# A transformer block on one core: which softmax quads VectorE computes, and the latencies the instruction order is planned with

## The chip, the cores and the metric

The kernel runs on one core of a Trainium2 chip. The metric is the device time of one execution in microseconds (us); less is better. The core has five engines that run side by side, each through its own instruction list in order, and they wait for each other on semaphores: TensorE (PE; its weight loads are listed as PEld), VectorE (DVE), ScalarE (ACT), GpSimd (POOL) and SyncE (SP), which mostly issues DMAs. PE writes its results to PSUM, eight banks of 128 x 512 floats.

## The reference

One pre-norm transformer block on a sequence of 2048 with 640 features, 32 heads of 20:

```python
qkv = layernorm(x) @ wqkv                     # 640 -> 3*640
p   = softmax(q @ k.T * 20**-0.5)             # 32 heads, 2048 x 2048 each
h   = x + (p @ v) @ wo
g   = layernorm(h)
out = h + (gelu(g @ w_gate) * (g @ w_up)) @ w_down   # 640 -> 1728 -> 640
```

The softmax needs 32 x 2048 x 2048 exponentials, and that sets the shape of the kernel.

## The kernel before, in words

**Tiles and slots.** Scores are made transposed, with 128 keys on the partitions. A *tile* is 128 x 512 scores (one PSUM bank); a *quad* is four tiles, one for each of four heads (`g` names the group of four heads, `j` the head in it). The queries are cut into eight chunks, of 512, then five of 256, then two of 128 (`SIZES`, line 316). A *slot* is 16 quads, 64 tiles: a head group at all keys for chunk 0, two groups for a chunk of 256, four for one of 128. There are 32 slots: 0 to 7 are chunk 0, 8 to 11 chunk 1, 12 to 15 chunk 2, 16 to 19 chunk 3, 20 to 23 chunk 4, 24 to 27 chunk 5, 28 and 29 chunk 6, 30 and 31 chunk 7.

**Two ways to an exponential.** Most tiles go to ACT: `unit` (line 941) makes the scores of two or three tiles on PE (L965), ACT takes the exponential of them in one instruction (L368, `pts` or `rege` from `ps`), and the quads are multiplied with v on PE (`pv_op`, line 922; in the trace L368, `ps` from `v_all`). Units of three and of two tiles alternate over banks 0 to 2 and 3 to 4. Some quads of each slot, `D_QUADS[slot]` (line 336), are computed on DVE by `d_exp` (line 867): each tile's scores are scaled to a 16-bit integer out of PSUM (L889), and then a group of two tiles ("l", 128 x 1024, slots below 18) or four tiles ("w", 128 x 2048, from slot 18, `D_WIDE`) goes through three one-input passes and two or three two-input passes of bit arithmetic. In the slots of `DA_SLOTS` the last addition is a DMA that accumulates, issued by POOL (line 910).

Which quads these are, and when DVE begins them, is set here:

```python
        n = D_QUADS[s_]
        taken = [quads[len(quads) * (m + 1) // (n + 1)] for m in range(n)]
        rest = [q + (j,) for q in quads if q not in taken for j in range(4)]
        part = D_PART if lead[s_] == 0 else 1.0
        dq += [(max(len(tiles) + ... - lead[s_], dq[-1][0] if dq else 0), q + (j,))
               for m, q in enumerate(taken) for j in range(4)]
```

The taken quads are spread over the slot, and each is begun `lead` (`D_LEAD`, line 338) ACT tiles ahead of its place.

**The rest of a chunk** (`post`, line 1083), once its attention is done: the attention output is transposed (by a DMA on SP, `dma_transposes`, line 621, except for chunk 0 and the last one), multiplied with wo (L667), added to x on DVE (L1105), normalized, transposed again, and put through the gate (PE L1138, copied out of PSUM on DVE by L1173), the gelu in place on ACT (L368, `rege` from `rege`), the up projection (PE L1138) times the gate (DVE L1187), and the down projection (PE L1218) plus h (DVE L1222). The gelu needs another activation table than the exponential, so ACT pauses its exponentials for a gelu, with a table load before and one after it. Chunk 1's gelu is kept for chunk 2's (`MERGE`). The last chunk takes another road (L1160, L1163), as nothing is left beside it.

**The order of the instructions** is written out when the kernel is built. Every operation is recorded with an engine, an estimated duration, an estimated latency (`lat`: from its end to when its result is seen) and a priority, and `Sched.schedule` (line 94) simulates the five engines with these estimates: whenever an engine is free it takes the ready operation of the best priority. Exponentials and their scores have priority 0, the background work (`post`, projections) a worse one. The order that comes out is each engine's program; on the chip each engine keeps that order whatever the real durations are. Where PE would be too little busy, the planner adds matmuls with zero weights (`self.pad`: L368, `ps` from `kt_all,zer`, in groups of four) or idle full-size ones (`self.warm`: `ps` from `kt_all`).

So a change of an estimate changes no work, only the order; a change of `D_QUADS` moves work between ACT and DVE, and the order too.

Of the kernel before, what the change touches and what calls it, by code (L numbers as in the profile page):

```python
# [46 lines left out]
class Sched:  # L47
# [13 lines left out]
    def op(self, eng, fns, dur, prio, reads=(), writes=(), acq=(), rel=(), after=(), sem=None, lat=None, mode=None, util=0.0):  # L61
        if eng == "dve" and rel and prio > self.ev:
            prio = self.ev
        o = Op()
        o.i = len(self.ops)
        o.eng, o.dur, o.lat, o.sem = eng, dur, DRAIN[eng] if lat is None else lat, sem
        o.util = util
        o.mode = mode
        o.tag = writes[0] if writes else None
        o.fns = fns if isinstance(fns, list) else [fns]  # L70
        o.prio = (prio, o.i)
        deps = set(after)
        for r in reads:
            if r in self.lw:
                deps.add(self.lw[r])
        for w in writes:
            if w in self.lw:
                deps.add(self.lw[w])
            deps.update(self.rd.get(w, ()))
        for r in reads:  # L80
            self.rd.setdefault(r, []).append(o.i)
        for w in writes:
            self.lw[w] = o.i
            self.rd[w] = []
        deps.discard(o.i)
        o.deps = deps
        o.acq = list(acq)
        o.rel = list(rel)
        o.succ = []
        o.ready = 0.0  # L90
        self.ops.append(o)
        return o.i
# [237 lines left out]
PV_QUADS = 2  # L330
D_LAG = 8
MERGE = (1,)
DA_ISSUE, DA_LAT = 0.95, 7.0
DA_SLOTS = (1, 2, 3, 5) + tuple(range(9, 32))
PR, PR2 = 12, 6
D_QUADS = (1,) + (2,) * 15 + (2, 2) + (3,) * 10 + (2, 2, 2, 2)
D_FIRST, D_PART = 2, 0.75
D_LEAD = ((0,) * 8, (0, 10, 20) + (42,) * 21)
D_WIDE = 18
RSQRT_MAGIC = float(0x5F3759DF)  # L340

# [1 line left out]
P_QK, P_PV, P_PRO, P_EPI, P_LN, P_BG = 0, 1, 1.5, 2, 2.5, 3  # L343
# [3 lines left out]
def bass_sequential_preLN__mha_block__glu_gated_geglu__prompt_kernel(  # L347
# [12 lines left out]
    with ExitStack() as es:  # L360
        sc = Sched(nc)
        op = sc.op
# [4 lines left out]
        def I(method, *args, **kwargs):  # L367
            return lambda eng: getattr(eng, method)(*args, **kwargs)  # L368
# [64 lines left out]
        wg = carve(NA * DFF).rearrange("p (a f) -> p a f", a=NA)  # L433
        wu = carve(NA * DFF).rearrange("p (a f) -> p a f", a=NA)
# [55 lines left out]
        def cst(fn, key, n=128):  # L490
# [7 lines left out]
           reads=["zer"], writes=["qf1"])  # L498
        op("act", I("activation", f32(qt_all[:, 2, :, :]), zer[:, 0:2].bitcast(FP32).to_broadcast([128, 2048]), ACT.Copy), 1.8, P_QK,
           reads=["zer"], writes=["qf2"])  # L500
        op("act", I("activation", v_all[:, :, :, DH], zer[:, 0:1].unsqueeze(2).to_broadcast([128, NT, H]), ACT.Copy, bias=1.0), 0.5, P_QK,
           reads=["zer"], writes=["vones"])
# [28 lines left out]
        def load(dst, src, key, mb, after=(), writes=None):  # L531
            return op("sp", I("dma_start", dst, src), 0.08, P_BG, writes=writes or [key], after=after,
                      sem=key, lat=mb)
# [85 lines left out]
                   rel=[bk], after=after)  # L619

        def dma_transposes(src, rkeys, dst, wkey, after=()):
            op("sp", I("dma_start_transpose", dst, src), 1.25, P_EPI, reads=rkeys, writes=[wkey], sem=f"xp{wkey[1]}", lat=2.0, after=after)

        _id = [0]

# [114 lines left out]
        def proj_q(t, c, banks, prio, evac="dve"):  # L740
            proj_qk(0, t, c, q_un[:, t, :], ("qu", t), banks, prio, evac)
            if t == 0 and c == 0:
                for j in range(4):
                    q_keys[0][0].append(("q", 0, 0, j))
                    dma(qt_all[32 * j + 1:32 * j + 21, 0, 0, :], q_un[DH * j:DH * j + DH, 0, :], ("q", 0, 0, j),
                        [("qu", 0), "qtm0"], "qc", 2.2, prio - 0.1)
            dma(qdr[c, 128 * t:128 * t + 128, :], q_un[:, t, :], ("qdr", c, t), [("qu", t)], f"qw{t}", 2.7,
                max(prio, P_BG) if t == 0 else prio, 0.4)
            w_readers.append(op("dve", I("tensor_scalar", aq[t].bitcast(I16), q_un[:, t, :].bitcast(I16), 0x7FFF, None,
                                         ALU.bitwise_and), 0.2, prio, reads=[("qu", t)], writes=[aqk(t)]))  # L750

        def q_bound(c, ts, g0, g1, banks, prio):
            bk = Bank(*banks)
            key = ("bk", sc_id())
            for k, t in enumerate(ts):
                w_readers.append(op("pe", lambda eng, k=k, t=t: eng.matmul(
                    bank(bk)[0:32, :], sel[:, t, :], aq[t], start=(k == 0), stop=(k == len(ts) - 1)),
                    c_mm(512), prio, mode="full", util=0.05, reads=[aqk(t), ("sel", t)], writes=[key],
                    acq=[bk] if k == 0 else []))
            op("dve", lambda eng: eng.tensor_scalar(qoff[0:32, :], bank(bk)[0:32, :], OFF, None, ALU.add), c_dve(512), prio,  # L760
               reads=[key], writes=["qoff"], rel=[bk])
            dma(odr[c], qoff[0:32, :], ("odr", c, g0), ["qoff"], "ow", 2.5, prio, 0.4)
            new = [("qo", c, g0)] + [("q", c, g0, j) for j in range(4)]
            for j in range(4):
                dma(qt_all[32 * j + 1:32 * j + 21, c, g0:g1, :],
                    qdr[c].rearrange("(g j e) s -> j e g s", j=4, e=DH)[j, :, g0:g1, :], ("q", c, g0, j),
                    [("qdr", c, t) for t in ts] + q_fills[c], f"q{c}{g0}", 2.5, prio, keep=False)
            dma(qt_all[0:128:32, c, g0:g1, :], odr[c].rearrange("(g j) s -> j g s", j=4)[:, g0:g1, :], ("qo", c, g0),
                [("odr", c, g0)] + q_fills[c], f"q{c}{g0}", 2.5, prio, keep=False)
            for g in range(g0, g1):  # L770
                q_keys[g][c] += new
# [36 lines left out]
        slot_end = []  # L808
        lead = sum(D_LEAD, ())
        for s_, (c, gs) in enumerate(slots):  # L810
            nk = 512 // CHUNKS[c][1]
            quads = [(s_, g, kb) for g in gs for kb in range(NT // nk)]
            n = D_QUADS[s_]
            taken = [quads[len(quads) * (m + 1) // (n + 1)] for m in range(n)]
# [258 lines left out]
        def prefetch(c):  # L1073
            q0, nq = CHUNKS[c]
            nt = nq // 128
            tb = base(c)
            op("sp", I("dma_start", h_sb[:, tb:tb + nt, :], x_hbm[q0:q0 + nq, :].rearrange("(t p) d -> p t d", p=128)), 0.08, P_EPI,
               writes=[("h", tb + tt, hf) for tt in range(nt) for hf in range(2)], sem=f"xr{c}", lat=2.0 + nq * 0.0034,
               after=tuple(e_ops) + tuple(w_readers) if c == 0 else ())
# [167 lines left out]
        for s_, (c, gs) in enumerate(slots):  # L1247
            if c == 0:
                g = s_
                if g + 1 in STEP:  # L1250
                    t, (g0, g1) = g + 1, STEP[g + 1]
                    pr = P_EPI if t == 1 else P_BG
                    proj_q(t, 0, BG0, pr)
                    proj_k(t, BG0, pr)
                    q_bound(0, (t - 1, t), g0, g1, BG0, pr)
                if g < 3:
                    for kt in range(NT * g // 3, NT * (g + 1) // 3):
                        proj_v(kt, 1, BG0, P_BG)
                if g == 5:
                    prefetch(0)  # L1260
                if g >= 5:
                    cc = g - 4
                    for t in range(NA):
                        proj_q(t, cc, BG0, P_BG)
                    q_bound(cc, tuple(range(NA)), 0, NG, BG0, P_BG)
                if g == 7:
                    wr = tuple(w_readers)
                    load(wg, B_w_gate.rearrange("(a p) f -> p a f", p=128), "wg", 11.0, after=wr)
                    load(wu, B_w_up.rearrange("(a p) f -> p a f", p=128), "wu", 16.0, after=wr)
                    load(wd[:, 0:NF - 1, :], B_w_down[0:(NF - 1) * 128, :].rearrange("(a p) d -> p a d", p=128),  # L1270
                         "wd", 21.0, after=wr)
                    r0 = (NF - 1) * 128 - F0[-1]
                    load(wd[r0:128, NF - 1, :], B_w_down[(NF - 1) * 128:DFF, :], "wd", 2.6, after=wr)
                    op(POOL, I("memset", wd[0:r0, NF - 1, :], 0.0), 0.8, P_BG, writes=["wdz", "pool"], after=wr)
            while ui < len(units) and begins[ui] < slot_end[s_]:
                unit(ui)
                ui += 1
            if gs[-1] == NG - 1:
                tail = c == len(CHUNKS) - 1
                sc.ev = P_EV  # L1280
                post(c, ALLB if tail else BGF[c + 1], ALLB if tail else BGC[c + 1], tail)
                if not tail:
                    prefetch(c + 1)
# [30 lines left out]
```

## Time and profile before

| | |
|---|---|
| runs before | 913.15, 915.69, 915.77 us; median 915.69 |
| the profiled execution | 915.13 us, of it the span from the first to the last instruction 913.0 us |
| busy | ACT 871.2 us (95%), PE 832.7 (91%), DVE 763.3 (84%), POOL 134.2 (15%) |
| exponentials on ACT | 356 of 128 x 1536 and 344 of 128 x 1024: 1756 tiles in 700 instructions |
| first exponential, end of the last one | 32.85 us, 876.26 us |
| mean granted TensorE clock | 0.994 of full speed |

A page of the profile has six parts; busy time is the time in which at least one instruction of the engine runs, and an engine that is off the path to the end may idle at no cost. Part 4 follows the chain of work that ended last back from the last instruction, and tells which engine holds it up. Other views give each engine's busy time in chosen stretches, or every instruction in order of time with the idle time before it and what ended it.

The kernel falls in three stages: the first 32 us (loads, first normalization and projections), the loop of exponentials to 876 us with all other work beside it, and a tail of 37 us, in which the last chunk goes through projection, gate, up and down, with what is left over of the chunks before it.

### The profile page before, as it was taken

How to read it: one execution, taken by the hardware profiler on the slowest of the kernel's cores; microseconds unless marked ns; L12 is line 12 of the kernel's file. 1: busy time of each engine (PE TensorE's matmuls, PEld its weight loads, DVE VectorE, ACT ScalarE, POOL GpSimd, SP SyncE). 2: the span in 40 equal slices, each digit the busy share in tenths (PEclk: the TensorE clock that was granted, in tenths of full speed). 3: DMA queues.
4: the chain of work that ended last, by engine and by line, in shares of the span. 5: the costliest groups of instructions: out<-in, count | busy, mean ns of one | idle time of the engine just before them, and what ended most of it. 6: DMA issues, size and time to landing. Idle time of an engine off the chain costs nothing.

```text
span 913.0 us, 25152 instructions
## 1 busy us (share of the span) xinstructions
PE 832.7 (91%) x11135; PEld 383.4 (42%) x11180; DVE 763.3 (84%) x1426; ACT 871.2 (95%) x786; POOL 134.2 (15%) x239
## 2 busy tenths in 40 slices
PE   3999999998897887899998989999999999999998
PEld 2432222222243332334443443344444445666667
DVE  8869989988798985777887989989999998958643
ACT  7999899999999999999999999999999999999971
POOL 5001110000013111111321101031102110203000
PEclk9999999999999999999999999999999999999999
DMA  7213344346304231242422324433353344314300
GB/s 259 84 31 79 79 87 108 96 96 203 127 1 76 48 59 24 48 68 59 91 51 50 64 39 85 91 62 71 78 107 62 70 81 98 47 26 85 56 9 23
DMA packets 52500, 68.05 MB, mean 75 GB/s; under 512 B 20892, under 2 KB 38392, under 8 KB 52392
## 3 DMA queue, kind: packets, MB, share of 16 engines
q0 software_dynamic: 12960, 33.56, 20.4%
q1 hardware_dynamic: 39432, 32.89, 13.2%
q8 instruction: 87, 1.43, 0.6%
q14 instruction: 21, 0.17, 0.1%
HBM read 20.12 MB, written 8.09 MB: 31 GB/s over the span
## 4 chain that ended last, share of the span: by engine, by line
ACT 68%; PE 19%; DVE 7%; DMA 2%; POOL 2%; issue 1%; SPq 0%
ACT pts L368 43%; ACT rege L368 24%; PE ps L965 5%; PE ps L667 4%; PE ps L1138 3%; PE ps L368 3%; PE ps L1218 3%; DMA regw<-in_A_wqkv_dram 1%; ACT L368 1%; DVE qt_all L368 1%; DVE rege L889 1%; DVE qt_all L889 1%; DVE dwx L368 1%; POOL nw L368 1%; DVE rege L368 1%
## 5 line engine op out<-in xcount | busy, mean ns | idle before, releaser
L368 ACT ACTIVATE pts<-ps 128x1536 bf16<-128x1536 f32 (+1 forms) x468 | 556.1, 1352 | 5.1 <-PE ps L965 2.7
L965 PE MATMUL ps<-qt_all,kt_all 32*128 32x256 bf16 (+2 forms) x4096 | 315.0, 274 | 42.6 <-ACT pts L368 25.5
L368 ACT ACTIVATE rege<-ps 128x1536 bf16<-128x1536 f32 (+1 forms) x232 | 289.7, 1359 | 5.5 <-PE ps L368 3.8
L965 PEld LDWEIGHTS ps<-qt_all,kt_all 32*128 32x128 bf16 x4096 | 108.6, 92 | 252.6 <-ACT pts L368 130.5
L1138 PE MATMUL ps<-rege,regw 128*128 128x256 bf16 (+2 forms) x1103 | 158.0, 274 | 9.6 <-DVE rege L1187 3.6
L368 PE MATMUL ps<-pts,v_all 128*21 128x256 bf16 (+2 forms) x2338 | 124.5, 276 | 0.4 <-ACT pts L368 0.3
L1138 PEld LDWEIGHTS ps<-rege,regw 128*128 128x128 bf16 x1120 | 85.9, 98 | 61.4 <-issue 27.0
L889 DVE TENSOR_SCALAR rege<-ps 128x512 int16<-128x512 f32 x120 | 82.3, 686 | 19.6 <-PE ps L965 18.7
L368 PE MATMUL ps<-rege,v_all 128*21 128x256 bf16 (+2 forms) x1358 | 91.8, 280 | 0.4 <-DVE rege L368 0.2
L889 DVE TENSOR_SCALAR qt_all<-ps 128x512 int16<-128x512 f32 x116 | 79.5, 686 | 12.0 <-PE ps L965 11.1
L667 PE MATMUL ps<-regw 128*128 128x512 bf16 (+1 forms) x345 | 84.2, 351 | 4.7 <-DMA regw<-in_A_wqkv_dram 1.6
L1218 PE MATMUL ps<-regw,rege 128*128 128x320 bf16 x448 | 78.1, 301 | 1.7 <-DVE rege L1222 0.8
L368 DVE TENSOR_TENSOR qt_all<-qt_all 128x2048 int16<-128x2048 f16 (+3 forms) x79 | 74.2, 940 | 1.0
L368 PEld LDWEIGHTS ps<-pts,v_all 128*21 128x21 bf16 x2338 | 53.9, 91 | 32.3 <-issue 26.9
L368 DVE TENSOR_SCALAR qt_all<-qt_all 128x2048 int16<-128x2048 int16 (+3 forms) x111 | 63.5, 574 | 1.0
L1187 DVE TENSOR_TENSOR rege<-rege,ps 128x512 bf16<-128x512 bf16 (+1 forms) x53 | 35.8, 678 | 23.7 <-PE ps L1138 21.8
L368 DVE TENSOR_TENSOR rege<-rege 128x1024 f16<-128x1024 f16 (+1 forms) x74 | 50.6, 684 | 0.9
L1218 PEld LDWEIGHTS ps<-regw,rege 128*128 128x128 bf16 x448 | 37.4, 97 | 30.5 <-issue 13.6
L368 DVE TENSOR_SCALAR rege<-rege 128x1024 int16<-128x1024 int16 (+2 forms) x112 | 48.3, 439 | 2.2 <-DMA rege<-qt_all 1.0
L368 PE MATMUL ps<-kt_all,zer 128*32 128x512 bf16 x576 | 49.5, 390 | 0.0
L667 PEld LDWEIGHTS ps<-regw 128*128 128x128 bf16 x360 | 28.1, 99 | 45.8 <-issue 24.4
L368 PEld LDWEIGHTS ps<-rege,v_all 128*21 128x21 bf16 x1358 | 36.0, 91 | 21.7 <-issue 14.2
(114 smaller groups left out, 785.4 us busy)
## 6 DMA issues: line engine op xcount, KB each, us to landing
qt_all<-qt_all POOLq DMA_DIRECT2D x11, 512.0 KB, 5.1
qt_all<-dwx POOLq DMA_DIRECT2D x11, 512.0 KB, 5.8
rege<-rege POOLq DMA_DIRECT2D x16, 256.0 KB, 3.6
rege<-dwx POOLq DMA_DIRECT2D x8, 512.0 KB, 5.3
dvx<-qt_all POOLq DMA_DIRECT2D x8, 512.0 KB, 4.6
rege<-in_A_x_dram SPq DMA_DIRECT2D x5, 640.0 KB, 5.8
q_rows<-regw SPq DMA_DIRECT2D x20, 128.0 KB, 1.9
out_dram<-rege SPq DMA_DIRECT2D x16, 160.0 KB, 2.6
```

The source lines that it names most:

```text
L368: return lambda eng: getattr(eng, method)(*args, **kwargs)
L667: yield op("pe", lambda eng, l=l, r=r, k=k: eng.matmul(bank(bk, n), l, r, start=(k == 0), stop=(k == len(steps) - 1)), c_mm(n) + cold, pri ...
L889: d_ops.append(op("dve", lambda eng: eng.tensor_scalar(v[:, 512 * h:512 * h + 512], bank(b), EXP_MUL, -32000.0, ALU.mult, ALU.max), c_dve( ...
L965: return lambda eng: eng.matmul(out()[:, kk * nq:(kk + 1) * nq], kt_all[32 * j:32 * j + 32, g, kt * 128:(kt + 1) * 128], qt_all[32 * j:32 ...
L1138: op("pe", lambda eng, a=a, f=f, fi=fi: eng.matmul(bank(bk)[:, fi * nq:(fi + 1) * nq], w[:, a, F0[f]:F0[f] + 128], hnT[:, a, 128 * tb:128 ...
L1187: hdone.append(op("dve", lambda eng, bu=bu, fv=fv, w=w: eng.tensor_tensor(fv, fv, bank(bu, w), ALU.mult), c_dve(w), p, reads=[ku] + hkeys( ...
L1218: op("pe", lambda eng, f=f, o=o, hf=hf, bk=bk: eng.matmul(bank(bk, 320), ha_f[:, o:o + 128], wd[:, f, hf * 320:(hf + 1) * 320], start=(f = ...
```

## The change

Fewer quads on DVE in slots 20, 23 and 26 (two in place of three), more in slots 12, 15, 28 and 30 (three in place of two): 74 quads in place of 73. From slot 11 on a quad is begun 39 tiles ahead, not 42. Four estimates of the planner change: the accumulating DMA lands after 6.4 (was 7.0), a DMA transpose 2.8 after its issue (was 2.0), the gate and up weights after 12.0 and 17.5 (were 11.0 and 16.0).

```diff
-DA_ISSUE, DA_LAT = 0.95, 7.0
+DA_ISSUE, DA_LAT = 0.95, 6.4
-D_QUADS = (1,) + (2,) * 15 + (2, 2) + (3,) * 10 + (2, 2, 2, 2)
+D_QUADS = (1,) + (2,) * 11 + (3, 2, 2) * 2 + (3, 3, 2) * 3 + (3, 3, 2, 3, 2)
-D_LEAD = ((0,) * 8, (0, 10, 20) + (42,) * 21)
+D_LEAD = ((0,) * 8, (0, 10, 20) + (39,) * 21)
@@ dma_transposes
-            op("sp", I("dma_start_transpose", dst, src), 1.25, P_EPI, ..., lat=2.0, after=after)
+            op("sp", I("dma_start_transpose", dst, src), 1.25, P_EPI, ..., lat=2.8, after=after)
@@ slot 7: the feed-forward weights
-                    load(wg, B_w_gate.rearrange("(a p) f -> p a f", p=128), "wg", 11.0, after=wr)
-                    load(wu, B_w_up.rearrange("(a p) f -> p a f", p=128), "wu", 16.0, after=wr)
+                    load(wg, B_w_gate.rearrange("(a p) f -> p a f", p=128), "wg", 12.0, after=wr)
+                    load(wu, B_w_up.rearrange("(a p) f -> p a f", p=128), "wu", 17.5, after=wr)
```

More of the change, by code (lines that the diff above doesn't have):

```diff
@@ L621, in dma_transposes @@
         def dma_transposes(src, rkeys, dst, wkey, after=()):
-            op("sp", I("dma_start_transpose", dst, src), 1.25, P_EPI, reads=rkeys, writes=[wkey], sem=f"xp{wkey[1]}", lat=2.0, after=after)
+            op("sp", I("dma_start_transpose", dst, src), 1.25, P_EPI, reads=rkeys, writes=[wkey], sem=f"xp{wkey[1]}", lat=2.8, after=after)
         _id = [0]
```

## The prediction

> **What bounds the kernel now.** I read the chain that ended last first, then the groups of instructions with shapes kept apart, busy time by stretches, and the timelines of ACT and PE at the end.
>
> The chain, then two rows of the groups (columns: count, busy us, mean ns of one, idle before):
>
> ```profile
> ACT 68%; PE 19%; DVE 7%; DMA 2%; POOL 2%; issue 1%; SPq 0%
> ```
>
> ```profile
> L368 ACT ACTIVATE pts<-ps 128x1536 bf16<-128x1536 f32 x235 | 364.2, 1563 | 3.6 <-PE ps L368 2.0 <-PE ps L965 1.3
> L368 ACT ACTIVATE pts<-ps 128x1024 bf16<-128x1024 f32 x233 | 262.8, 1139 | 1.5 <-PE ps L965 1.5
> ```
>
> ACT's exponentials are the path. One tile costs 1563 - 1139 = 424 ns more in an instruction; with the fixed part, five tiles (a three and a two) start every 2.26 us, 0.452 a tile. Busy time by stretches (columns: stretch, its length, busy time and count of each engine):
>
> ```profile
> 347.00:457.00 110.00, 99.84 (x1270) 42.43 (x1275) 83.17 (x167) 109.94 (x97) 17.64 (x30) 1.00 0.32 58
> ...
> 597.00:738.00 141.00, 134.43 (x1929) 63.14 (x1929) 137.13 (x216) 139.66 (x123) 25.62 (x46) 1.00 0.40 77
> 738.00:800.00 62.00, 59.53 (x1134) 35.59 (x1133) 54.90 (x92) 61.94 (x55) 11.84 (x21) 1.00 0.40 75
> 800.00:861.00 61.00, 59.31 (x1397) 38.15 (x1401) 41.60 (x70) 60.66 (x54) 9.62 (x19) 1.00 0.31 60
> ...
> 877.00:913.00 36.00, 31.59 (x393) 25.73 (x390) 14.29 (x35) 10.31 (x14) 0.00 (x0) 1.00 0.05 20
> ```
>
> In all four stretches of the loop ACT is busy over 99%. DVE is full in the third quarter (137.1 of 141) and has room before it (83.2 of 110) and after it (41.6 of 61). The tail is PE's: 31.6 of 36, ACT 10.3. ACT's and PE's timelines there:
>
> ```profile
> 873.84 2.42 ACT L368 ACTIVATE rege<-ps 128x1536 bf16<-128x1536 f32 x2
> 876.28 1.28 ACT L368 ACT_TABLE_LOAD   x1
> ...
> 881.39 1.70 ACT L368 ACTIVATE rege<-rege 128x1792 bf16<-128x1792 bf16 x1 [2.31 <-DVE rege L1173]
> ```
>
> ```profile
> 874.58 3.29 PE L1138 MATMUL ps<-rege,regw 128*128 128x256 bf16 x32
> 877.80 0.23 PE L368 MATMUL ps<-pts,v_all 128*21 128x128 bf16 x3
> ...
> 894.61 3.97 PE L1218 MATMUL ps<-regw,rege 128*128 128x320 bf16 x28
> 898.42 7.25 PE L1138 MATMUL ps<-rege,regw 128*128 128x128 bf16 x127
> ```
>
> The last exponentials end at 876.26. Chunk 6's gelu (1792 wide) runs only at 881.39, and its up and down projections and a part of chunk 5's stand on PE before the last chunk's 127 gate and up matmuls can begin at 898.42. So the feed-forward work that DVE delayed in its full stretch is paid in the tail, where PE has nothing else beside it.
>
> **The change, part by part.** The built order of each engine tells what moves.
>
> *Exponentials.* 74 quads for 73: 1752 tiles on ACT, again in 700 instructions (the last one holds a single tile). 4 x 0.424 = **-1.7 us** on the path.
>
> *Chunk 6's gelu.* Before, ACT pauses for gelus after 679, 1049, 1419, 1596 and 1736 tiles, and once more behind the last. After: 681, 1098, 1403, 1546 and 1726, and chunk 6's now stands in the pause at 1726. The 1.70 us, less 0.1 overlap with the one ahead (two take 3.28 where their means, 1904 and 1467 ns, make 3.37), go onto the path: **+1.6**. Two table loads vanish, both in the tail, where ACT afterwards waited 2.31 and 3.82 us for DVE: nothing.
>
> *The tail.* Behind the last scores PE has 25 fewer matmuls of 256 columns (chunk 5's up projection), 20 fewer of 128 and one fewer L1218. Paces: (7.25 - 0.22) / 126 = 0.056 for 128 columns; (3.29 - 0.22 - 6 x 0.056) / 25 = 0.109 for 256; (3.97 - 0.30) / 27 = 0.136 for 320. 25 x 0.109 + 20 x 0.056 + 0.136 = **-4.0**. Would the last chunk's own chain of steps hold the tail instead? From its last value product (ends 878.43) to its gates PE took 20.2 us before, and 17 after by the matmuls gone from that part. The steps between (DVE copy 0.69, transposes 0.66, reciprocal and scaling 0.95, transposes 0.45, ACT copy 0.70, wo 1.5, DVE add, statistics and casts 2.4, square root 0.2, scaling 0.6, transposes 0.45, ACT copy 0.70) make 9.3, some 11 with hand-overs. So PE keeps the tail.
>
> *From the loop to the tail.* The last scores are issued as the last exponential but one begins. Five tiles were then left, now four, so this point moves by three tiles and the gelu: -1.3 + 1.6 = +0.3. The fourth tile counts nothing: PE has 13 L1218 and 10 L1138 (2.3 us) between the last scores and the last value products, more than the 1.6 that the exponentials need (1.3 from a three-tile one to the next, 1.139 - 0.424 = 0.7 for one tile, the first begun 0.4 ahead of the scores). So far 0.3 - 4.0 = **-3.7**.
>
> *PE's room.* The 4.0 us must fit in the loop. The order has 56 fewer zero matmuls (14 groups at 0.22, the step from x4, 0.39, to x8, 0.61) and four more idle full-size ones (0.22 each at 512 columns): 3.1 - 0.9 = 2.2 us over the loop. In the last third of the tiles alone, 23 groups fewer (27 for 50): 5.1 us. Cover enough there.
>
> *DVE.* Two more narrow quads and one wide fewer. Narrow: four L889 at 0.686, and twice three passes of 0.42 and two of 0.685: 8.0 us. Wide: 2.74 + 3 x 0.69 + 2 x 1.22 = 7.3. In all +8.7 us, none of it on the path: slots 12 to 15 lie at about 347 to 457, where DVE idles 27 us for +16; slots 20, 23, 26 lie at 560 to 720, where 22 us go out of the full stretch; slots 28 and 30 come to 740 to 861, where it idles 26.5 for +14.5. If that cover failed, the late quads would hold their slot's last value products, and 1 us late would be 1 us.
>
> *Estimates and lead.* No instruction is added but three accumulating DMAs on POOL (0.93 us each; POOL is busy 15%) and their transfers. Accumulations of 512 KB landed 4.6 to 5.8 us after issue. Transposes landed after 3.3 on median, against 1.25 + 2.0 planned, so half of them came later than the order expects: at 289.71 PE had waited 1.00 us for one, and ACT then 0.66. Planned 0.8 later, that wait should go: **-0.7**, between nothing and 1.0; next there is DVE's copy of the gate (PE waits 0.39 at 293.82). But the order is dealt anew from slot 2 on, and with it ACT's losses. From 32.85 to 876.26 are 843.4 us; 1756 x 0.452 = 793.7, ten loads 12.8, gelus 23.3: **13.6 us** are lost; the longest wait is 2.77, ahead of 95.34, and five are 0.8 to 1.05 (at 199, 302, 570, 595, 598). What the new order loses no row shows. Bounds: these six gone (-7.5), or as much again (+7.5); I take 0, as both orders come from one planner, and keep some half of it each way for the range.
>
> Sum: -3.7 - 0.7 = -4.4 against the profiled execution, 915.13 - 4.4 = 910.7. That execution lay 0.56 below the median, so **911.3**.
>
> **Rivals.** (1) *PE has no room.* From 738 to 861 PE is busy 118.8 of 123. If what left the tail only delays scores, the 4.0 come back: 915.3. Against it: the zero matmuls given up there. (2) *The losses are dealt worse.* Three more waits of 1 us than now, like those at 199 and 302: 914.3. For it: each slot end needs DVE's copy of the sums (L368 `osb`) before the next slot's products, and DVE gets more quads. (3) *Slower: the clock.* At 565 to 570 and 590 to 600 the granted clock falls to 0.70, 0.59 and 0.73, full speed around them, in stretches where ACT idles 0.70, 0.97 and 1.01. A halved clock thus costs ACT time, and the change takes out 23 of 50 groups of zero matmuls in the last third, where PE, at 97%, has no slack: 3.4 us at half speed would cost 1.7 there. Faster by 4.4, and 2.75 to be seen: over four such spells (7.2 / 1.7) the kernel is measurably slower, and six give 921.5. Against it: real matmuls stand in the place of the zero ones, and before, the last third kept 1.00 throughout.
> [...]
>
> **Chances.** Forecast, 907 to 912.9: 0.55. Rival 1: 0.10. Rival 2: 0.18. Rival 3: 0.17. A measurement of this kernel can tell 0.3%, 2.75 us, from no change: faster (below 912.9) 0.55, same 0.28 (rivals 1 and 2), slower (above 918.4) 0.17. Range: 4.3 below (some half of the losses gone) and 6.7 above, which takes in rivals 1 and 2 and ends at rival 3's edge: 907 to 918.
>
> **What would show it.** ACT: 1752 tiles, chunk 6's gelu in the last pause, the last exponential ending near 875.5, and from there to the end 33 us, not 36.7; DVE below 90% from 597 to 738. Wrong: ACT waiting for PE's scores over 13.6 us in all; a granted clock under 1.00 behind 740; the last gates waiting on ACT or DVE and not on PE's queue; the pause at 1726 waiting for DVE's copies (L1173).

## The result, and the profile after

| | before | after |
|---|---|---|
| median (range), runs | 914.51 us (912.45 to 916.16), 17 | 918.91 us (913.99 to 926.34), 17 |
| ratio of after to before | | 1.0056, interval 1.0039 to 1.0073 |
| profiled execution, its span | 915.13, 913.0 | 926.34, 924.4 |
| mean granted clock | 0.994 | 0.980 |
| end of the last exponential, tail | 876.26, 36.7 | 892.38, 32.0 |

The kernel became measurably slower, not faster. The profiled execution of after is the longest of its 17 runs, so what follows shows the loss at its largest. Ratios in this document leave out a kernel's runs over 1.5% above its fastest; only `lat_only` below has such runs, five of its 12.

The chain that ended last in after:

```profile
ACT 59%; PE 27%; DVE 8%; DMA 2%; POOL 2%; issue 1%
```

ACT carries 59% of the chain where it carried 68%; PE has 27 for 19. The groups of ACT's exponentials (count, busy us, mean ns of one, idle before):

```profile
L368 ACT ACTIVATE pts<-ps 128x1536 bf16<-128x1536 f32 x236 | 362.0, 1551 | 8.8 <-PE ps L965 5.9 <-PE ps L368 2.0
L368 ACT ACTIVATE pts<-ps 128x1024 bf16<-128x1024 f32 x233 | 259.4, 1127 | 1.9 <-PE ps L965 1.9
L368 ACT ACTIVATE rege<-ps 128x1536 bf16<-128x1536 f32 x117 | 181.0, 1556 | 13.7 <-PE ps L965 9.0 <-PE ps L368 4.5
```

The row of before for the third group, which stands beside the two shown ahead of the result:

```profile
L368 ACT ACTIVATE rege<-ps 128x1536 bf16<-128x1536 f32 x121 | 187.8, 1566 | 5.4 <-PE ps L368 3.8 <-PE ps L965 1.3
```

The exponentials themselves are no slower. The idle time ahead of them has grown, and most of it ends with scores (L965): ACT waits for PE. By stretches (stretch, length, busy time and count of PE, PEld, DVE, ACT, POOL, granted clock, DMA share, GB/s):

```profile
347.00:457.00 110.00, 97.44 (x1207) 38.96 (x1209) 88.18 (x177) 104.46 (x91) 21.42 (x34) 0.94 0.31 57
...
597.00:738.00 141.00, 129.25 (x1761) 61.30 (x1763) 124.45 (x200) 132.48 (x116) 23.51 (x43) 0.96 0.38 66
738.00:800.00 62.00, 56.56 (x939) 31.13 (x936) 53.81 (x83) 61.17 (x53) 6.71 (x7) 1.00 0.42 77
800.00:861.00 61.00, 58.83 (x1421) 38.49 (x1420) 51.85 (x91) 59.57 (x53) 8.48 (x25) 0.97 0.36 73
...
893.00:924.40 31.40, 27.92 (x355) 22.88 (x353) 13.20 (x32) 6.15 (x11) 0.00 (x0) 1.00 0.06 22
```

DVE is relieved as planned (124.5 of 141 from 597, 88%), yet ACT idles 5.5 us from 347 and 8.5 from 597, where before it idled 0.1 and 1.3, and in the same stretches the clock is 0.94 and 0.96 where it was 1.00. At the two places where ACT lost most against before, two things come together: an engine that waited for a DMA, and matmuls at half clock. The first such place, in the timeline:

```profile
422.28 0.90 POOL L368 DMA_DIRECT2D rege<-qt_all  x1 [3.63 <-DVE qt_all L368]
...
428.80 0.43 DVE L368 TENSOR_SCALAR rege<-rege 128x1024 int16<-128x1024 int16 x1 [1.52 <-DMA rege<-qt_all]
...
430.20 0.48 DVE L1105 TENSOR_TENSOR rege<-ps,rege 128x320 bf16<-128x320 f32 x1
...
430.74 0.39 PE L965 MATMUL ps<-qt_all,kt_all 32*128 32x256 bf16 x2 [1.12 <-DVE rege L1105]
...
432.01 2.41 ACT L368 ACTIVATE pts<-ps 128x1536 bf16<-128x1536 f32 x2 [0.58 <-PE ps L965]
```

An accumulating DMA issued at 422.28 lands 6.5 us later; a load of x and a store of the output, issued at 422.42 and 422.83, are under way beside it. DVE stands 1.52 us at the operation that needs it, in its fixed order; the residual add (L1105) behind it comes late, PE waits 1.12 us for that, and ACT 0.58 for PE. So far a loss of half a microsecond. Then:

```profile
430.00:435.00 5.00, 3.69 (x47) 1.75 (x47) 5.00 (x11) 3.84 (x4) 0.86 (x1) 0.78 0.32 56
435.00:440.00 5.00, 5.00 (x41) 1.94 (x41) 2.41 (x7) 2.68 (x3) 0.86 (x1) 0.50 0.07 12
```

From 432.8 the clock is halved, for 13.7 us. PE is now full with 41 matmuls in 5 us, and ACT is busy 2.68 of 5. The 1.5 us of DVE have become 6.5 us on ACT between 432 and 447. The second place:

```profile
627.88 0.88 POOL L368 DMA_DIRECT2D qt_all<-dwx  x1 [1.62 <-DVE dwx L368]
627.97 4.71 SPq L368 DMA_TRANSPOSE rege<-o_nat  x2
...
637.50 1.29 DVE L368 TENSOR_SCALAR qt_all<-qt_all 128x2048 int16<-128x2048 int16 x2 [1.71 <-DMA qt_all<-dwx]
...
638.29 0.37 PE L1138 MATMUL ps<-rege,regw 128*128 128x256 bf16 x1 [4.09 <-DMA rege<-o_nat]
...
640.31 1.45 ACT L368 ACTIVATE rege<-ps 128x1536 bf16<-128x1536 f32 x1 [4.30 <-PE ps L965]
```

An accumulation of 512 KB and two transposes are issued within 2.8 us. The accumulation lands after 9.60 us, the transposes after 9.76 and 7.53. PE stands at the gate of L1138 with the next scores queued behind it, 4.09 us, and ACT 4.30; the clock is halved from 637.6, within PE's wait, for 10.2 us. In all ACT lost 29.5 us between its exponentials, where the same reckoning gives 12.9 for before (the time from the first start to the last, less ACT's other work and 0.063 us + 0.427 a tile for each exponential). That is 16.6 of the 16.9 us by which the last exponential ended behind the forecast.

### The profile page after: what moved, and what is told of

It reads as the page before. It is cut to its first block, busy times and chain, and to the rows that moved or that the text cites. A ratio compares the mean times of both kernels' runs of the same rounds, so it can differ in the third digit from the quotient of the medians.

```text
span 924.4 us, 25074 instructions
## 1 busy us (share of the span) xinstructions
PE 839.0 (91%) x11081; PEld 387.5 (42%) x11128; DVE 771.1 (83%) x1445; ACT 868.8 (94%) x784; POOL 130.4 (14%) x242
## 4 chain that ended last, share of the span: by engine, by line
ACT 59%; PE 27%; DVE 8%; DMA 2%; POOL 2%; issue 1%
ACT pts L368 37%; ACT rege L368 20%; PE ps L965 8%; PE ps L1138 5%; PE ps L368 5%; PE ps L667 5%; PE ps L1218 3%; DVE qt_all L368 2%; DMA rege<-o_nat 2%; DVE qt_all L889 1%; DVE dwx L368 1%; DMA rege<-qt_all 1%; ACT L368 1%; POOL nw L368 1%; PE ps L1057 1%
## 5 line engine op out<-in xcount | busy, mean ns | idle before, releaser
L965 PE MATMUL ps<-qt_all,kt_all 32*128 32x256 bf16 (+2 forms) x4096 | 316.8, 276 | 40.7 <-ACT pts L368 21.4
L368 ACT ACTIVATE rege<-ps 128x1536 bf16<-128x1536 f32 (+1 forms) x230 | 285.6, 1346 | 14.7 <-PE ps L965 10.0
L965 PEld LDWEIGHTS ps<-qt_all,kt_all 32*128 32x128 bf16 x4096 | 109.9, 92 | 250.4 <-ACT pts L368 121.9
L1138 PE MATMUL ps<-rege,regw 128*128 128x256 bf16 (+2 forms) x1105 | 158.5, 275 | 15.5 <-DMA rege<-o_nat 4.4
L1138 PEld LDWEIGHTS ps<-rege,regw 128*128 128x128 bf16 x1120 | 86.4, 98 | 66.5 <-issue 30.1
L889 DVE TENSOR_SCALAR rege<-ps 128x512 int16<-128x512 f32 x124 | 84.8, 684 | 17.8 <-PE ps L965 17.0
L667 PE MATMUL ps<-regw 128*128 128x512 bf16 (+1 forms) x344 | 83.0, 349 | 4.2 <-ACT regw L615 1.8
L1218 PE MATMUL ps<-regw,rege 128*128 128x320 bf16 x448 | 80.9, 306 | 1.5 <-DVE qt_all L889 1.0
L368 DVE TENSOR_TENSOR qt_all<-qt_all 128x1024 int16<-128x1024 f16 (+3 forms) x81 | 74.3, 917 | 1.0
L889 DVE TENSOR_SCALAR dvx<-ps 128x512 int16<-128x512 f32 x56 | 38.4, 685 | 12.6 <-PE ps L965 12.4
L667 PEld LDWEIGHTS ps<-regw 128*128 128x128 bf16 x360 | 28.4, 98 | 44.6 <-issue 22.8
L368 POOL DMA_DIRECT2D qt_all<-dwx x25 | 23.4, 937 | 165.1 <-DVE dwx L368 152.0
```

The lines of the kernel that those rows point to most:

```text
L667: yield op("pe", lambda eng, l=l, r=r, k=k: eng.matmul(bank(bk, n), l, r, start=(k == 0), stop=(k == len(steps) - 1)), c_mm(n) + cold, pri ...
L889: d_ops.append(op("dve", lambda eng: eng.tensor_scalar(v[:, 512 * h:512 * h + 512], bank(b), EXP_MUL, -32000.0, ALU.mult, ALU.max), c_dve( ...
L965: return lambda eng: eng.matmul(out()[:, kk * nq:(kk + 1) * nq], kt_all[32 * j:32 * j + 32, g, kt * 128:(kt + 1) * 128], qt_all[32 * j:32 ...
L1138: op("pe", lambda eng, a=a, f=f, fi=fi: eng.matmul(bank(bk)[:, fi * nq:(fi + 1) * nq], w[:, a, F0[f]:F0[f] + 128], hnT[:, a, 128 * tb:128 ...
L1218: op("pe", lambda eng, f=f, o=o, hf=hf, bk=bk: eng.matmul(bank(bk, 320), ha_f[:, o:o + 128], wd[:, f, hf * 320:(hf + 1) * 320], start=(f = ...
```

## The experiments

Theory A: the work moved as forecast; the new order lets DMAs meet, engines stand at them, and the waits also halve PE's clock. Rivals: **fill**, the missing zero matmuls let the clock fall; **estimates**, the planner's latencies were merely too short, and longer ones would repair the order; **order alone**, the new order loses its time without any late DMA. "Half clock" of a run is worked out as 2 x (1 - mean clock) x span; a "spell" is a stretch in which the granted clock is 0.50.

**1 and 2: late DMAs taken out, the order kept.** `after_da8` and `before_da8` let each accumulating DMA move an eighth of its columns (the rest of the last addition is left out).

```diff
-I("dma_start", v, di, accum_op=ALU.add)
+I("dma_start", v[:, 0:64 * n], di[:, 0:64 * n], accum_op=ALU.add)
```

> The changed kernel with its order kept, each accumulating DMA cut to an eighth of its columns (the rest of the last addition of the DVE quads is left out). Late-DMA theory: the 9.6 and 9.8 us landings at 628 come from an accumulation and two transposes in flight together, PE then stands 4.1 us at the gate and DVE 8.8 us in all at accumulations, and the clock falls behind these waits. Then the median drops to 909 to 913, the spread of the runs from 12 us to under 4, the mean clock rises to 0.994 or more, the waits of PE and DVE on DMAs fall under 2 us. Clock theory: the order has too little PE work in places whatever the DMAs do: clock 0.98 to 0.993, median 916 to 920, spread near 12. Quad theory (DVE overloaded late): median 916 to 920, ACT's losses at the slots with more quads.

> The kernel before with the same cut of its accumulating DMAs to an eighth. Late-DMA theory: before waits only 3.9 us on DMAs in its loop, so 1 to 3 us faster than before (912 to 914); the difference to the changed kernel with the cut is then the prediction's own sum, -3.7. Clock theory: within 1 us of before, clock 0.994.

After 910.33 (906.65 to 916.14, 12 runs), ratio to before 0.9962 (0.9945 to 0.9979); before 914.24 (912.35 to 915.44, 11), 0.9999 (0.9989 to 1.0009). The cut gains 8.6 us on the new order and 0.3 on the old. Between the medians of the two with the same cut lie 3.9 us, close to the forecast's sum of the work, 3.7; between their three runs each at a clock of 1.000 lie 5.1 (907.3 and 912.4 in the middle). The profiled execution of `after_da8`, the fastest of its 12 runs, in two of the stretches:

```profile
347.00:457.00 110.00, 99.59 (x1298) 40.20 (x1290) 93.53 (x192) 109.90 (x96) 22.46 (x34) 1.00 0.14 21
...
597.00:738.00 141.00, 132.52 (x1832) 63.72 (x1830) 127.77 (x205) 139.39 (x122) 24.52 (x43) 1.00 0.15 22
```

With the same instructions in the same order the clock stays 1.00 and ACT idles 0.1 and 1.6 us. Over the whole program it loses 10.1 by the reckoning above. "Order alone" falls: the loss goes with the transfers, the order kept. That the accumulations' traffic merely slows the engines falls too, as the same cut gives the old order nothing and DVE's one-input passes over 128 x 1024 (`rege`) take 419 ns on average in after and in `after_da8`. Half clock is not gone in every run: `after_da8` has 8.2 us of it on average, after 18.2, and its runs still spread over 9.5 us, where under 4 had been expected.

**9 and 16: transposes alone, and both.** `after_xp1` keeps one of five blocks of each DMA transpose (four fifths left out); `after_xp1da8` has both cuts.

```diff
-I("dma_start_transpose", dst, src)
+I("dma_start_transpose", dst[:, 0, :], src[:, 0:128])
```

> The changed kernel with its order kept, each DMA transpose cut to one of its five blocks (the other four are left out, so four fifths of the activations behind it are stale). Accumulations are whole. If transposes in flight beside accumulations are what lands late: TensorE's waits for transposes vanish (4.4 us to under 0.5), clock 0.996 or more, 908 to 912, like the kernel with the cut accumulations. If the accumulations alone are late: VectorE still waits 5 to 8 us for them, spells stay, 914 to 919.

> The changed kernel with its order kept and both cuts, accumulations to an eighth and transposes to a fifth. Late-DMA theory: no spell left but such as come from TensorE's own thin places, median 906 to 909, close to the 906.7 that the kernel with cut accumulations reaches in its runs at full clock.

`after_xp1` 913.62 (909.32 to 920.42, 12), 0.9994 (0.9971 to 1.0017); `after_xp1da8` 908.78 (907.53 to 911.35, 6), 0.9952 (0.9936 to 0.9967). The transposes alone give 5.3 of the 10.1 us back. In the profile of `after_xp1`:

```profile
347.00:457.00 110.00, 96.61 (x1189) 38.68 (x1199) 88.61 (x177) 104.14 (x91) 20.82 (x30) 0.94 0.30 55
...
597.00:738.00 141.00, 132.16 (x1847) 63.63 (x1846) 131.01 (x210) 139.58 (x123) 25.68 (x44) 1.00 0.33 64
```

The place behind 628 is healed, the one behind 428, which waited for an accumulation, is not (ACT idles 5.9 us). These two spells go with the DMA that stood ahead of them. The spell at 511, with no wait close ahead, went too. DVE had waited 3.21 us for an accumulation 13 us before it; in `after_da8` that wait is gone, but in `after_xp1` DVE still waits 2.15 us there and no spell follows. The median missed the 908 to 912 that theory A gave for this run.

**5 and 6: the fill.** Each planned group of four zero matmuls becomes eight in `after_fill2` and one in `before_fill0` (432 zero matmuls fewer); the order stays.

```diff
-for j in range(4)]
+for j in (0, 1, 2, 3) * 2]     # after_fill2;  for j in (0,)]  in before_fill0
```

> The changed kernel with its order kept and every group of zero matmuls doubled, eight for four (520 more zero matmuls, 28 us of TensorE by 0.22 a group, mostly where it would idle). Fill theory: the fill that the change took out is what keeps the clock; mean clock 0.996 or more, 909 to 914. Late-DMA theory: the spells at half clock begin behind waits for DMAs (at 428.8 and 634), which stand at the head of TensorE's queue where no fill is; the clock hardly rises, 915 to 921.

> The kernel before with its order kept and one zero matmul in place of each group of four (432 fewer). Fill theory: spells of half clock in many places, clock under 0.985, 920 or more, the more so as this takes out eight times what the change took out. Late-DMA theory: the fill matters little beside the waits; within 3 us of before.

`before_fill0` 914.58 (912.73 to 916.71, 12), 1.0002 (0.9990 to 1.0013), with its two spells where before has them (567 and 591). `after_fill2` 925.57 (925.08 to 927.18, 4), 1.0125 (1.0105 to 1.0145), slower than either theory gave: a spell at 638 stays, behind the same gate's wait for the transpose (1.91 us). The spells at 430 and 511 are gone from its profile, and its half clock is 9.2 us on average, where after has 18.2. Yet nothing is gained: ACT's many losses of 0.05 to 0.5 us between exponentials add up to 15.2 us for 9.6, as they would if the added matmuls stood in the scores' way. So three quarters of the old order's fill could go without harm, and "fill" as the cause of the loss falls; whether more fill can hold the new order's clock up stays open.

**3 and 4: which part of the change.** `ql` is before with the new `D_QUADS` and lead 39; `lat_only` is before with the four new estimates. (The new quads with lead 42 run out of the planner's buffers for DVE's exponentials, so these two edits belong together. The weights' two estimates do nothing: with 11.0 and 16.0 put back, the changed order is the same instruction for instruction.)

> The kernel before with the new quads and the lead of 39, all four estimates as before. Quad theory: slow as the changed kernel, 917 to 920. Late-DMA theory: accumulations and transposes meet by the luck of the order, so anything from 910 to 918, and its waits on DMAs tell which; the tail is short (33 us) in any case.

> The kernel before with the four new estimates alone (accumulation 6.4, transpose 2.8, weights 12.0 and 17.5). Late-DMA theory with the estimates guilty: DVE waits on accumulations that land later than planned, 916 to 920, more spread than before. Quad theory: within 2 us of before (912.5 to 916.5), tail near 37 us.

`ql` 918.22 (914.02 to 921.22, 9), 1.0044 (1.0027 to 1.0062). `lat_only` 925.7 (914.65 to 933.8, 12), 1.0080 (1.0048 to 1.0112). Each part alone makes an order that is slower; so their sum explains nothing. In `ql` PE waits 1.55 us ahead of 675.12 and 2.76 ahead of 780.84 for transposes that wo (L667) needs, and spells of 6.8 and 10.2 us begin within these waits. `lat_only` is slower than any theory gave and has 32 us of half clock in the median of all its runs. The clock row of its profile's page shows where (tenths of full speed, 40 slices of 23 us):

```profile
PEclk9999999999999999999999999789997779999999
```

**15: the same cut on the worst order.** `lat_only_da8` is `lat_only` with accumulations cut to an eighth.

> The kernel before with the four new estimates (the slowest of the single parts) and its accumulating DMAs cut to an eighth, order kept. If late accumulations are behind its 51 us of half clock: half clock under 15 us and 912 to 917. If its spells come from POOL's and TensorE's own work: 922 to 928 as without the cut.

917.33 (914.22 to 921.03, 12), 1.0040 (1.0027 to 1.0053): half clock falls from 32 to 10 us in the median. By the medians of all runs 8.4 us come back; by the ratios it is 3.7 us, with intervals that touch. A is supported here, not more. In the profile of `lat_only` only the first spell (590) has a late DMA close ahead: PE waits 1.75 us at L667 and goes on 0.09 us after a load of x has landed, 5.3 us after its issue and beside an accumulation. Two spells are left in `lat_only_da8`: the one at 704 stands behind DVE waiting 1.15 us for POOL, the one at 741, 10.2 us long, behind waits of PE for DVE of half a microsecond. A wait needn't be a DMA's.

**7 and 8: longer estimates.** Accumulations 9.0 and transposes 5.0, with the new quads (`after_slack`) and the old (`before_slack`).

```diff
-DA_ISSUE, DA_LAT = 0.95, 6.4        # transposes: lat=2.8
+DA_ISSUE, DA_LAT = 0.95, 9.0        # transposes: lat=5.0
```

> The changed quads and lead, the order built with landings as late as the slow ones of the traces: the accumulation after 9.0 (not 6.4), a transpose after 5.0 (not 2.8). Late-DMA theory: TensorE and VectorE wait under 3 us for DMAs, clock 0.996 or more, 908 to 912, spread under 6 us, so faster than before. Quad theory: 916 to 920 as the changed kernel. Fill theory: by the luck of the fill, no gain to be expected, 915 to 920.

> The old quads and lead with the same late landings, 9.0 and 5.0. Late-DMA theory: the kernel before waits little already, so 911 to 915, and the kernel with the new quads and the same landings is 3 to 4 us faster than this one (its tail). Quad theory: this one is the faster of the two by 3 us or more.

925.46 (924.65 to 929.7, 5), 1.0138 (1.0115 to 1.0161), and 920.95 (920.36 to 922.4, 5), 1.0079 (1.0063 to 1.0096). I expected a gain and was wrong. `before_slack` ran at full clock throughout and is still slower: ACT waits for the last value products at the ends of slots. As I read it, the planner obeys the late estimate and places them behind it. In `before_slack`:

```profile
96.98 2.37 ACT L368 ACTIVATE rege<-ps 128x1536 bf16<-128x1536 f32 x2 [4.03 <-PE ps L368]
```

Three such places (ahead of about 97, 125 and 154) make 10.9 us of the 21.6 that it loses; before loses 3.1 at the first of them. Full clock is thus no proof of a good order.

**10, 11, 12, 14: single estimates, and fewer accumulations.** `da64_only` and `xp28_only` are before with one new estimate each; `after_xp20` is after with the transposes' old one; `after_dve` is after with the last addition of slots 9 to 17 done on DVE in place of POOL's DMA (`DA_SLOTS` without them).

> The kernel before with the accumulation's estimate alone at 6.4. Late-DMA theory with this estimate guilty: VectorE stands at accumulations and spells follow, 918 to 926 like all four estimates together. If the transposes' estimate is guilty: 912.5 to 916.

> The kernel before with the transpose's estimate alone at 2.8. By my prediction's step the wait at 289.71 goes: 0.7 us faster, 913 to 914. If a small change of any estimate deals the order anew with losses of its own, as the bound of 7.5 us allows: anywhere from 910 to 922, and mostly slower, as the order before is a picked one.

> The changed kernel with the last addition of the DVE quads done on VectorE in slots 9 to 17, not by an accumulating DMA (28 groups... of 1024 columns, 0.68 us each on VectorE, where it has room; the late slots keep their DMAs). Late-DMA theory: the spell near 430 goes, the one near 630 can stay, 913 to 919. A version that beats both would be under 912.

> The changed kernel with the transpose's estimate alone put back to 2.0. If the estimate of 2.8 protects: more waits of TensorE for transposes than the changed kernel's 4.4 us, 918 to 924. If it is one more dealing of the order: anywhere from 911 to 922, by its waits.

`da64_only` 913.48 (12 runs), 0.9997 (0.9985 to 1.0009), though in its profile PE waits 2.97 us for a transpose at 794.73 and DVE 2.64 for an accumulation at 492.90: one spell of 3.4 us follows the first, none the second. So late DMAs by themselves don't make an order slow. Together with the transposes' estimate, harmless alone too, it makes `lat_only`. `xp28_only` 914.55 (11), 1.0018 (1.0000 to 1.0035): PE's waits for transposes were gone, as the forecast had it, and there was no gain. `after_dve` 916.7 (12), 1.0042 (1.0016 to 1.0068): no spell near 430, new ones at 617, 750 and 787, and 5.4 us of PE waiting for transposes at L667. `after_xp20` 917.19 (8), 1.0047 (1.0022 to 1.0072).

**13, 17, 18: one estimate in small steps.** After with `DA_LAT` 7.0, 6.7 and 7.3 in place of 6.4.

```diff
-DA_ISSUE, DA_LAT = 0.95, 6.4
+DA_ISSUE, DA_LAT = 0.95, 7.0        # after_da67: 6.7;  after_da73: 7.3
```

> The changed kernel with the accumulation's estimate alone put back to 7.0. If that estimate is what makes the changed order meet its DMAs: 911 to 914, with VectorE's waits on accumulations under 3 us. If any new order brings waits of its own: 914 to 922, the waits at other places.

> The changed kernel with the accumulation's estimate half way, 6.7. If the estimate acts as slack (later planned, fewer waits met), between the changed kernel and the one with 7.0: 911 to 917. If each order's losses are dealt anew with no trend: anywhere from 909 to 922.

> The same with 7.3. Slack theory: waits for DMAs as few as with 7.0, 909 to 913. Dealt anew: anywhere from 909 to 922, with waits at new places.

| `DA_LAT` | 6.4 (after) | 6.7 | 7.0 | 7.3 |
|---|---|---|---|---|
| median us | 918.91 | 920.85 | **910.66** | 924.47 |
| range | 913.99 to 926.34 | 918.66 to 929.95 | 910.23 to 912.45 | 921.55 to 935.27 |
| ratio to before | 1.0056 | 1.0101 (1.0067 to 1.0136) | 0.9969 (0.9958 to 0.9981) | 1.0134 (1.0095 to 1.0173) |

With 7.0 the kernel beats both, at the time that was forecast. Its profile has no wait on a DMA in the loop, one spell (622, 6.8 us) behind a wait of DVE for POOL, its last exponential ends at 876.27, and the third quarter reads

```profile
597.00:738.00 141.00, 135.26 (x1806) 64.53 (x1795) 126.69 (x202) 136.32 (x119) 25.37 (x43) 0.98 0.40 71
```

I took this at first for "0.6 us more slack is enough". 7.3 is slower by 14 us, even beyond the 909 to 922 that I allowed for any order, so that reading falls, and "estimates" with it: 7.0 is one good order among neighbours, not the end of a trend.

**What the runs say together.** Within one program, time follows half clock. A straight line through each kernel's runs gives:

| kernel | us per us of half clock | time at full clock | mean half clock | mean time |
|---|---|---|---|---|
| before (115 runs) | 0.27 | 912.4 | 6.4 us | 914.1 us |
| after (17) | 0.39 | 912.3 | 18.2 | 919.3 |
| `after_da8` (12) | 0.38 | 907.3 | 8.2 | 910.4 |
| `after_da7` (6) | 0.27 | 910.5 | 1.8 | 911.0 |
| `lat_only` (12) | 0.36 | 913.8 | 34.0 | 926.1 |

At full clock after equals before, by extension of its line (none of its runs was at 1.000; the standard error of that end is 0.7 us). There the late DMAs cost the new order 5.0 us directly (912.3 - 907.3), which eats the 5.1 us that it gains with the cut at full clock. The difference of the means, 919.3 - 914.1 = 5.2 us, is then the halved clock: 0.39 x 18.2 = 7.1 us for after, 0.27 x 6.4 = 1.7 for before. Against its own cut order after loses 8.9 us in the mean (919.3 - 910.4): 5.0 directly, and some 4 by more half clock. That the late accumulations cost the new order its gain is shown by the cut. That a wait sets off each spell is only the likeliest reading, as one spell began with no wait close ahead and some waits passed without a spell.

## Why the prediction was wrong, step by step

- *Exponentials, and chunk 6's gelu:* right. 1752 tiles; ACT's timeline has the gelu at the pause, and it waited for nothing:

```profile
873.00 1.28 ACT L368 ACT_TABLE_LOAD   x1
874.30 4.87 ACT L368 ACTIVATE rege<-rege 128x2048 bf16<-128x2048 bf16 x3
```

- *The tail:* right, 32.0 us where 33 were expected and 36.7 were before. After the last gelu's feed-forward work PE goes on as forecast:

```profile
906.01 3.97 PE L1218 MATMUL ps<-regw,rege 128*128 128x320 bf16 x28
909.81 7.25 PE L1138 MATMUL ps<-rege,regw 128*128 128x128 bf16 x127
```

- *PE's room and DVE:* right as far as the runs reach. With the accumulations early the -3.7 appeared as -3.9 between the medians, -5.1 between the runs at full clock, so the work fitted in the loop. Rival 1 (no room) falls.
- *Transposes' estimate, -0.7:* not confirmed. Alone it removed PE's waits for transposes and gave 1.0018 (1.0000 to 1.0035), because ACT loses as much elsewhere in the order that it makes.
- *"But the order is dealt anew from slot 2 on ... I take 0":* **the step that failed.** 16.6 us were lost more in the profiled execution, 7.6 in the median (918.91 against 911.3; 8.8 if the forecast -4.4 is set against before's median of 17 runs), over the bound of 7.5 that I had worked out and twice the half of it that I kept. I had counted the six longest waits of the old order as the measure of what a new one could lose. Late DMAs put 5.0 us of direct waits into the new order, by the lines above, and the bound had no term for the half clock that came with them, some 4 us more: at the first place 1.5 us of DVE became 6.5 us of ACT.
- *Rival 3:* it named the state of the engine that did the damage, a halved clock, but for a cause that fell (missing fill) and in a place that stayed nearly clean (behind 740 one spell of 3.4 us, against 34 us between 430 and 650). *Rival 2*, losses dealt worse, was nearest in its cause; its price, three waits of 1 us, was too small, and what it named for it, DVE's copy of the sums, was not what held PE up at the two places. Rival 3's price, 1.7 us for 3.4 at half clock (before's spell at 567 lasted 3.41), was an estimate that no run shows; it was too high beside the measured 0.39.
- *Estimates and lead:* the accumulations "landed 4.6 to 5.8 us after issue" was a median by kind. What held the engines up at the two places were later ones, 6.5 beside other transfers and 9.6 beside two transposes.

What stays open: why a spell began at 511 with PE busy 4.75 of the 5 us ahead of it; why equal waits are followed by a spell in one run and not in another; and what makes one order good and its neighbour bad before it is run. By the estimates alone nothing told 7.0 from 6.7 or 7.3.

## What to carry to other kernels

A change that makes a planner write the order anew is two changes: the work, which can be reckoned from rows to within a microsecond or two (here 3.7 forecast, 3.9 to 5.1 measured), and a new draw of the order, which here was worth from 910 to 925 us between neighbouring estimates; the second needs a range as wide as runs of several neighbours make it. Look in such an order for transfers that will be under way together and for what stands behind their readers in program order, and separate the two parts by shrinking the transfers with the order kept. Judge by many runs, with the granted clock beside each time.

## What the runs showed of the hardware

- **Transposes beside accumulations.** In after, seven DMA transposes that met no accumulation in flight landed after 2.6 to 2.7 us; nineteen that met one took 2.6 to 9.8. Accumulations had a median of 4.0 and a longest of 9.6. With the accumulations cut to an eighth no transpose took over 4.8.
- **Half clock can begin behind short waits.** In after the spell at 433 began behind waits of 1.52 us (DVE) and 1.12 (PE), with PE busy 3.69 of the 5 us from 430; in `ql` one began within a wait of PE of 1.55, in `after_fill2` within 0.5 us behind one of 1.91; at 511 PE had been busy 4.75 of 5. Not each such wait is followed by one: before's PE wait of 1.00 at 289.71 was not. In the loops of the two profiles the spells lasted 3.41 and 6.83 us (before, from 566.99 and 590.88) and 13.65, 10.24, 10.24 and 3.41 (after, from 432.81, 511.31, 637.61 and 838.99): one to four times 3.41.

  No run shows what a wait must be like to be followed by a spell, nor why the 17 runs of after, one order, have from 7 to 37 us of half clock and spread over 12 us. In the loop of after PE's longest wait was the 4.09 us at 638, and no other was over 1.50; in before a spell began at 567 with PE busy 4.21 of the 5 us ahead. The price that the table shows, 0.27 to 0.39 us for one of half clock, is below the 0.5 of rival 3's estimate (1.7 for 3.4), which would fit ACT, not PE, being the bound in part of a spell.
- **Zero matmuls can be worth nothing.** 432 fewer changed nothing in before (1.0002, 0.9990 to 1.0013). Twice as many in after went with less half clock (9.2 us for 18.2 on average, 4 and 17 runs) and a slower kernel (1.0125).
